# Two attention layers on one core: the readers of a projection's PSUM bank in another order, and one round of an input tile moved ahead

## Chip, cores and metric

One NeuronCore of a Trainium2 chip runs the whole program. The metric is device time in microseconds (us), from the launch to the end of one execution. TensorE is called PE here, VectorE DVE, ScalarE ACT, GpSimd POOL and SyncE SP, as in the profile.

## What is computed

Two attention layers over 2048 tokens, width 576, 32 heads of 18, whose outputs stand side by side. Layer A has one key head and one value head for all 32 query heads and attends to all tokens. Layer B is cut into four segments of 512 tokens. It attends causally inside a segment and adds what a linear memory of the earlier segments gives. A learned gate for each head mixes the two.

```python
def _A_ref(x, wq, wk, wv, wo):
    scores = einsum("bhqd,bkd->bhqk", q, k) * Dh ** -0.5
    o = einsum("bhqk,bkd->bhqd", softmax(scores), v)
    return o.reshape(B, S, H * Dh) @ wo

def _B_ref(x, wq, wk, wv, wo, beta):
    phi = lambda t: where(t > 0, t + 1.0, exp(t))
    g = sigmoid(beta)
    for s in range(4):                                   # segments
        a_dot = softmax(qs @ ks.T * scale + mask) @ vs   # causal
        a_mem = (phi(qs) @ M) / (phi(qs) @ z + 1e-6)
        o = g * a_mem + (1.0 - g) * a_dot
        M = M + phi(ks).T @ vs
        z = z + phi(ks).sum(over tokens)
    return o @ wo
```

## The kernel before

The program has two parts. The first, up to about 281 us, makes the projections: for A four chunks of 512 tokens (c), for B four segments (s). The second is the attention with the output projections. It walks through blocks of heads of A and B, and ACT makes the exponentials there.

**Tiles and rings.** A projection's output (heads times 18 rows, 512 tokens) is cut into five tiles t of up to 126 rows. PE makes a tile in one PSUM bank `pj` out of a ring of four, with 14 matmuls, since every operand is split in two fp32r parts (`wh`, `wl` and `xh`, `xl`) (proj, L252 to L259). Other PSUM names: `nd` (two banks, first half of the values), `tr` (one bank, transposes), `mm` (one bank, small sums).

**The readers of a bank.** In B's key tiles (L444 to L472) a bank has five readers, and the framework lets only one engine at a time read it. Before, they come in this order: DVE's maximum `kmB` (L454), ACT's copy `qp` (L124 in split2), DVE's subtraction that makes the second part of `qp` (L125), ACT's ramp, a Relu of the negated tile (L403 in phi), and, after ACT's exponential of it (L404), DVE's sum that makes the features `kf` or `qf` (L406). PE then transposes the features (`natural`, L422, tile `tr`) and DVE copies them out (L423).

**Weights that are still being loaded.** Segment 0 does something more in its key tiles: the last five parts (10 to 14) of B's weights, those of the query projection, are split there. In tile t, ACT rounds part 10 + t out of its buffer `wr` (L249 in split_wpart), POOL subtracts (L250), and POOL then issues the load of the next part (L240 in load_wpart):

```python
if s == 0:
    split_wpart(10 + t)
    if t < 4:
        load_wpart(11 + t)
```

All five steps are held in program order on their engines (`pin`, which is tc.keep_in_program_order). So the load of part 11 + t stands on POOL's queue behind POOL's subtraction of part 10 + t, and that stands behind ACT's rounding of part 10 + t.

**The gate.** Behind the fifth part POOL issues seven small loads of the gate's argument `gt` (L479). ACT takes its exponential (L550), and DVE finishes it (L551 to L553).

**What sets the order.** In the first part, what is not pinned is put in order by the framework's scheduler when the program is built. Each engine then runs its fixed list from the front and waits at the first instruction whose inputs are not there. The attention part has an order written out by hand.

**The next segment's x.** `next_x` and `load_xk` (L199 to L219) load and round the next segment's input: in segment 0 on DVE (`behind=True`: cast, then subtraction), in segments 1 and 2 on ACT and POOL (`aside=True`). Three buffers `xr` hold the raw input.

Of the kernel before, what the change touches and what calls it, by code (L numbers as in the profile page):

```python
# [14 lines left out]
ALU = mybir.AluOpType  # L15
AX = mybir.AxisListType
# [61 lines left out]
def attention_pair_kernel(ctx, tc, a_xT, a_w, a_wo, b_xT, b_w, b_wo, b_beta, ident_d, hmask_d, bmask_d, cmask_d, sel_d, zmask_d, selx_d, sely_d, out):  # L78
    nc = tc.nc
# [37 lines left out]
    fm = cp.tile([128, 5], F32, name="fm")  # L117
    nc.gpsimd.memset(fm, 0.0)

    def split2(pool, src, R, hold=lambda ins: ins):  # L120

        n = src.shape[-1]
        qp = pool.tile([128, 2, C], F32R, name="qp", bufs=3)
        hold(nc.scalar.copy(qp[:R, 0, :n], src))  # L124
        hold(nc.vector.tensor_tensor(qp[:R, 1, :n], src, qp[:R, 0, :n].bitcast(F32), op=ALU.subtract))  # L125
        return qp

    def store_parts(qp, r0, R, dst, h0, nh):
        nc.sync.dma_start(dst[h0 : h0 + nh].rearrange("h d j t -> (h d) j t"), qp[r0 : r0 + R].bitcast(F32))
# [30 lines left out]
    with ExitStack() as ph:  # L160
# [109 lines left out]
        for c in range(NCH):  # L270
            ready = {}
            if c == 0:

                for k in range(5):
                    load_part(raw[0][:, k, :CA], a_w, 0, CA, k, nc.sync)
                    load_part(xraw(0, k), a_xT, 0, C, k, nc.sync if k else nc.scalar)
                for k in range(5):
                    load_part(xraw(1, k), a_xT, C, C, k, nc.sync)
                nc.sync.dma_start(ident, ident_d)
                xh, xl, fillx = next_x(a_xT, 0)  # L280
                nx = next_x(a_xT, 1)
                for t in TILES:
                    ready[t] = ps.tile([128, C], F32, name="mm", bufs=1) if t == 3 else ps.tile([128, C], F32, name="pj", bufs=4)
                for k in range(5):
                    fillx(k)
                    split_w(wAh, wAl, raw[0][:, k, :CA], 0, CA, k, nc.vector)
                    parts_ = [(wAh, xh), (wAh, xl), (wAl, xh)] if k < 4 else [(wAh, xh), (wAl, xh)]
                    for i, (w, x) in enumerate(parts_):
                        for t in TILES:
                            M = 114 if t == 4 else 126  # L290
                            nc.tensor.matmul(  # L291
                                ready[t][:M],
                                w[:, k, 126 * t : 126 * t + M],
                                x[:, k],
                                start=k == 0 and i == 0,
                                stop=k == 4 and i == 1,
                            )
                for k in range(5):
                    nx[2](k)
            else:  # L300
                xh, xl = nx[:2]
                nx = next_x(a_xT, c + 1) if c < NCH - 1 else next_x(b_xT, 0)
                if c == 2:
                    wBl, wBh = (pw.tile([128, 5, WB], F32R, name=n) for n in ("wBl", "wBh"))
            for t in TILES:
                M = 114 if t == 4 else 126
                if c == 0:
                    pj = ready[t]
                else:

                    nm, bufs = ("nd", 2) if c == 1 and t == 4 else ("pj", 4)
                    pj = ps.tile([128, C], F32, name=nm, bufs=bufs)
                    proj(pj[:M], wAh, wAl, xh, xl, 126 * t, M)
                R = RT[t]
                if t == 4:
                    nc.vector.tensor_reduce(km[:M, c : c + 1], pj[:M], axis=AX.X, op=ALU.max, apply_absolute_value=True)
                    vT = p1.tile([128, C], F32, name="vT", bufs=2)
                    nc.scalar.copy(vT[96:114], pj[96:114])
                if t == 0:

                    pv = ps.tile([128, 4, 128], F32, name="tr", bufs=1)
                    for i in range(4):
                        nc.tensor.transpose(pv[:, i, 0:DH], vT[96:114, 128 * i : 128 * i + 128], ident[96:114, 96:114])
                    nc.vector.tensor_copy(VAv[:, 4 * c : 4 * c + 4, 1:VW], pv[:, :, 0:DH])
                nc.scalar.activation(AQ[:R, t, c * C : c * C + C], pj[:R], AF.Abs)
                R2 = 90 if t == 4 else 126
                if (c, t) == (NCH - 1, 3):
                    lastq = pj
                else:
                    qp = split2(pt, pj[:R2], R2)  # L330
                    store_parts(qp, 0, R, qA[c], H0[t], HT[t])
                if c == 0:
                    load_part(xraw(2, t), a_xT, 2 * C, C, t, nc.sync)
                if c:
                    nx[2](t)

                i = 5 * (c - 2) + TILES.index(t)
                if i >= 0:
                    split_wpart(i)
                    if i + 4 < 10 or i == 8:  # L340
                        load_wpart(i + 4 if i < 8 else 10)
                if t == 4:
                    nc.sync.dma_start(kA[:, :, c * C : c * C + C], qp[72:90].bitcast(F32))
            if c == 0:
                for i in range(4):
                    load_wpart(i)
                pin(nc.gpsimd.dma_start(hmask[:126], hmask_d))
                pin(nc.gpsimd.dma_start(bmask[:126], bmask_d))
                pin(nc.gpsimd.dma_start(sel[:114], sel_d))
                pin(nc.gpsimd.dma_start(zmask[:126], zmask_d))  # L350
                pin(nc.gpsimd.dma_start(selx[:126], selx_d))
                pin(nc.gpsimd.dma_start(sely, sely_d))
                pin(nc.gpsimd.dma_start(ones_d.rearrange("j (a b) -> (j a) b", b=128), onest))
# [43 lines left out]
        nc.gpsimd.memset(mz, 0.0)  # L397
        zc = p2.tile([128, 5], F32, name="zc")

        def phi(src, R, nm, bufs, hold=lambda ins: ins):  # L400

            e = p2.tile([128, C], F32, name="ph_e", bufs=2)
            hold(nc.scalar.activation(e[:R], src, AF.Relu, scale=-1.0))  # L403
            hold(nc.scalar.activation(e[:R], e[:R], AF.Exp, scale=-1.0))  # L404
            f = p2.tile([128, C], F32, name=nm, bufs=bufs)
            hold(nc.vector.scalar_tensor_tensor(f[:R], src, 0.0, e[:R], op0=ALU.max, op1=ALU.add))  # L406
            return f

        for s in range(NSEG):
# [34 lines left out]
            for t in range(5):  # L444
                if s == t == 0:
                    pj = ahead
                else:
                    pj = ps.tile([128, C], F32, name="pj", bufs=4)
                    proj(pj[:126], wBh, wBl, xh, xl, 630 + 126 * t if t < 4 else 504, 126)
                if t and not last:  # L450
                    natural(f, pkN[:, t - 1, :, 0:126], 0, 126)

                hold = (lambda ins: ins) if last else pin
                hold(nc.vector.tensor_reduce(kmB[:126, t : t + 1], pj[:126], axis=AX.X, op=ALU.max, apply_absolute_value=True))  # L454
                qp = split2(pt, pj[:126], 126, hold)
                if t < 4:
                    store_parts(qp, 0, 126, kB[s], 7 * t, 7)
                    hold(nc.vector.tensor_scalar(kbB[:126, t], zmask[:126, t], kmB[:126, t : t + 1], None, op0=ALU.mult))
                else:
                    store_parts(qp, 0, 72, qB[s], 28, 4)  # L460
                    store_parts(qp, 72, 54, kB[s], 28, 3)
                    magnitude(4, pj)
                if not last or t == 4:
                    f = phi(pj[:126], 126, "kf" if t < 4 else "qf", 2 if t < 4 else 5, hold)
                    if t == 4:
                        fs[4] = f
                if s and not last:
                    nx[2](t, aside=True)
                if s == 0:
# [3 lines that stand above are left out]
# [59 lines left out]
            if not last:  # L532
                for i in range(4):
                    values(i, 1)

            for t in range(4):
                pj = ps.tile([128, C], F32, name="pj", bufs=4)
                proj(pj[:126], wBh, wBl, xh, xl, 126 * t, 126)
                magnitude(t, pj)
                qp = split2(pt, pj[:126], 126)  # L540
                store_parts(qp, 0, 126, qB[s], 7 * t, 7)
                if s == 0:
                    nx[2](t, behind=True)
                    if t == 3:
                        nx[2](4, behind=True)
                if s:
                    fs[t] = phi(pj[:126], 126, "qf", 5)
                    from_memory(t)
                if (s, t) == (1, 1):
                    nc.scalar.activation(gt, gt, AF.Exp, scale=-1.0)  # L550
# [970 lines left out]
```

## Time and profile before

| what | value |
|---|---|
| device time, median of 3 runs | 1398.94 us (1397.28 to 1399.08) |
| device time of the profiled execution | 1397.32 us |
| its span, first to last instruction | 1395.4 us |
| PE busy in the span | 1382.5 us (99%) |
| ACT busy in the span | 1204.4 us (86%) |
| DVE busy in the span | 1033.2 us (74%) |
| POOL busy in the span | 261.1 us (19%) |
| granted PE clock | 0.999 |

About 1.9 us of the time lies outside the span. Matmuls are pipelined and overlap in the rows, so a busy PE means only that the next matmul had begun before the one ahead had drained. The step from one start to the next is what a matmul costs. A bracket at the end of a timeline row tells how long the engine sat idle before the instruction and who released it. An x14 at the end of a row means so many instructions in one row.

### The profile page before, as it was taken

To read this page: it belongs to the slowest core of one execution; us is meant where nothing else is said; L and a number is where in the kernel's file an instruction comes from. 1 tells how busy PE (TensorE), PEld (TensorE's weight loads), DVE (VectorE), ACT (ScalarE), POOL (GpSimd) and SP (SyncE) were. 2 spreads that over 40 slices of the span, in tenths; PEclk is the share of its full clock that TensorE was granted. 3 is DMA by queue.
4 is the path that set the end of the run, shared out by engine and by line. 5 is a ranking of instruction groups with operands and counts; after the bars stand their busy time and mean duration, and the time that the engine had idled before them with its cause. 6 is when DMAs were issued, how large, how long until landed. Compare 5 with 4: busy or idle time off the path is not lost.

```text
span 1395.4 us, 41198 instructions
## 1 busy us (share of the span) xinstructions
PE 1382.5 (99%) x17455; PEld 835.6 (60%) x17455; DVE 1033.2 (74%) x1512; ACT 1204.4 (86%) x1494; POOL 261.1 (19%) x382
## 2 busy tenths in 40 slices
PE   9999999999999999999999999999999999999998
PEld 6787887755554555555555555555555555555558
DVE  6655454477787788787888877876879778887884
ACT  4543553499999999999999999999999999999992
POOL 2443221003312211412110122113010220001002
PEclk9999999999999999999999999999999999999999
DMA  9766656576465445332312452232103321120013
GB/s 288 259 216 196 191 178 206 175 210 189 146 182 172 139 149 158 101 113 78 112 59 71 141 160 56 91 115 83 52 34 94 111 76 39 32 73 21 18 63 133
DMA packets 89022, 173.67 MB, mean 124 GB/s; under 512 B 12308, under 2 KB 20621, under 8 KB 88402
## 3 DMA queue, kind: packets, MB, share of 16 engines
q1 hardware_dynamic: 81902, 159.22, 36.6%
q0 software_dynamic: 2176, 6.51, 1.6%
q10 hardware_dynamic: 4752, 5.23, 1.1%
q8 instruction: 139, 2.28, 0.7%
q14 instruction: 53, 0.43, 0.1%
HBM read 99.65 MB, written 70.67 MB: 122 GB/s over the span
## 4 chain that ended last, share of the span: by engine, by line
PE 88%; DVE 5%; ACT 4%; issue 2%; DMA 1%; SPq 0%; POOL 0%; DVEq 0%; ACTq 0%
PE O L938 32%; PE E L890 20%; PE F L741 11%; PE pj L259 11%; ACT P L908 4%; PE E L898 3%; PE nd L496 2%; PE pj L496 2%; DVE W L905 2%; PE E L1222 2%; PE pj L291 1%; PE F L797 1%; PE tr L422 0%; DVE sm L690 0%; DMA stB<-qB 0%
## 5 line engine op out<-in xcount | busy, mean ns | idle before, releaser
L908 ACT ACTIVATE P<-E 128x1024 f32<-128x1024 f32 (+1 forms) x800 | 788.1, 1076 | 1.6 <-PE E L890 1.3
L905 DVE COPY W<-E 128x1024 f32<-128x1024 f32 (+2 forms) x416 | 453.2, 1089 | 143.1 <-PE E L890 84.2
L938 PE MATMUL O<-P,VA 128*32 128x256 f32 x7504 | 507.1, 379 | 0.0
L908 ACT ACTIVATE P<-W 128x1024 f32<-128x1024 f32 (+1 forms) x330 | 369.9, 1121 | 6.3 <-DVE W L905 5.6
L938 PEld LDWEIGHTS O<-P,VA 128*32 128x32 f32 x7504 | 259.0, 110 | 137.7 <-issue 4.3
L890 PE MATMUL E<-xl,kstA 56*128 56x512 f32 x1920 | 317.2, 430 | 2.1 <-ACT P L908 1.9
L890 PEld LDWEIGHTS E<-xl,kstA 56*128 56x128 f32 x1920 | 155.0, 184 | 159.1 <-issue 94.8
L913 POOL TENSOR_SCALAR_AFFINE_SELECT P<-P 128x256 f32<-128x256 f32 (+1 forms) x192 | 95.0, 495 | 412.5 <-ACT P L908 403.3
L725 POOL TENSOR_TENSOR xh<-xh,rb 126x512 f32<-126x512 f32 (+1 forms) x55 | 72.9, 1350 | 425.9 <-DVE PD L871 185.1
L741 PE MATMUL F<-woB,xh 126*32 126x192 f32 (+1 forms) x1920 | 126.6, 338 | 0.0
L938 PE MATMUL O<-PD,VA 128*32 128x256 f32 x688 | 88.9, 379 | 0.0
L741 PEld LDWEIGHTS F<-woB,xh 126*32 126x32 f32 (+1 forms) x1920 | 38.6, 108 | 74.9 <-issue 69.9
L938 PE MATMUL O<-P,vseg 128*32 128x256 f32 (+2 forms) x1536 | 81.4, 344 | 0.1
L947 DVE COPY oe<-O 128x512 f32<-128x512 f32 x64 | 44.3, 692 | 42.3 <-PE O L938 40.4
L259 PE MATMUL pj<-xh,wBl 128*126 128x512 f32 x180 | 71.9, 400 | 0.4 <-issue 0.4
L864 DVE TENSOR_SCALAR PD<-E 128x512 uint32<-128x512 f32 x86 | 59.2, 688 | 17.6 <-PE E L890 15.8
L259 PE MATMUL pj<-xh,wBh 128*126 128x512 f32 x180 | 71.6, 398 | 0.5 <-DVE xh L219 0.5
L124 ACT CAST qp<-pj 126x512 fp32r<-126x512 f32 (+1 forms) x54 | 31.1, 585 | 46.9 <-DVE kmB L454 41.8
L741 PE MATMUL F<-woA,xh 126*32 126x192 f32 (+1 forms) x960 | 63.9, 338 | 0.0
L938 PEld LDWEIGHTS O<-P,vseg 128*32 128x32 f32 x1536 | 48.8, 109 | 24.4 <-issue 1.9
L898 PE MATMUL E<-stB 56*128 56x256 f32 (+3 forms) x512 | 61.5, 348 | 2.0 <-ACT P L908 1.5
L871 DVE SCALAR_TENSOR_TENSOR PD<-PD,q 128x512 f32<-128x512 f32 x86 | 59.5, 692 | 3.0
(228 smaller groups left out, 1544.0 us busy)
## 6 DMA issues: line engine op xcount, KB each, us to landing
stB<-kB SPq DMA_DIRECT2D x96, 144.0 KB
stB<-qB SPq DMA_DIRECT2D x32, 288.0 KB
xl<-qA SPq DMA_DIRECT2D x30, 288.0 KB
oA<-oe SPq DMA_DIRECT2D x32, 256.0 KB
oB<-oe SPq DMA_DIRECT2D x32, 256.0 KB
qA<-qp SPq DMA_DIRECT2D x16, 504.0 KB
kB<-qp SPq DMA_DIRECT2D x16, 504.0 KB
qB<-qp SPq DMA_DIRECT2D x16, 504.0 KB
```

What stands on the lines that cost most here:

```text
L259: nc.tensor.matmul(dst, w[:, c0 : c0 + M], x, start=i == 0, stop=i == len(ops) - 1)
L496: nc.tensor.matmul(pj[:, :n], x, w, start=m == 0, stop=m == len(ops) - 1)
L725: ins = tc.keep_in_program_order(nc.gpsimd.tensor_tensor(dst, a, b, op=op))
L741: nc.tensor.matmul(dst[32 * j : 32 * j + 32], parts[ab, c][: RT[t], t, r0 : r0 + 32], wo[ab][: RT[t], t, c0 : c0 + n], start=start, stop=stop,
L864: v.tensor_scalar(y, e, EXP_A, EXP_B, op0=ALU.mult, op1=ALU.add)
L871: lambda: stt(p, p, POLY[3], w, op0=ALU.add, op1=ALU.mult),
L890: nc.tensor.matmul(e[:, j], kstA[rows, 128 * kt : 128 * kt + 128], st[rows, h, :], start=True, stop=True)
L898: nc.tensor.matmul(e[:, j, c0 : c0 + 512 - 128 * k], st[rows, 4 + h, ks], st[rows, h, 128 * k :], start=True, stop=True)
L905: gate.append(nc.vector.tensor_copy(src[:, hs, :n], e[:, hs, :n]))
L908: nc.scalar.activation(p[:, hs, :n], src[:, hs, :n], AF.Exp, scale=SCALE)
L913: nc.gpsimd.affine_select(diag, diag, pattern=[[0, 2], [0, m], [1, 128]], base=0, channel_multiplier=-1, compare_op=ALU.is_ge, fill=0.0)
L938: nc.tensor.matmul(o[32 * j : 32 * j + 32, q0 : q0 + n], v, p[:, j % 2, p0 : p0 + n], start=m == hf == 0, stop=last and hf == 1,)
```

## The change

Three things are moved, and no instruction is added or taken away.

1. The readers of a bank in B's key tiles come in the order copy, ramp, subtraction, features, maximum. The ramp (now in a function `negative`) is issued between copy and subtraction through a hook in split2. Tile 4 and the query tiles of segments 1 to 3 get the same order of copy, ramp, subtraction, features; ACT's absolute value (`magnitude`) stays ahead of the copy in the query tiles and behind the subtraction in tile 4. The last segment's key tiles 0 to 3 have no features; there only the maximum moves behind the split.
2. In A's tile 4 the maximum `km` comes after copy and subtraction.
3. In segment 0 the next segment's x is rounded one tile sooner: tile 0 ahead of the loop over query tiles, tile t + 1 in turn t.

```diff
+    def split2(pool, src, R, hold=lambda ins: ins, between=lambda: None):
...
         hold(nc.scalar.copy(qp[:R, 0, :n], src))
+        between()
         hold(nc.vector.tensor_tensor(qp[:R, 1, :n], src, qp[:R, 0, :n].bitcast(F32), op=ALU.subtract))
...
                 if t == 4:
-                    nc.vector.tensor_reduce(km[:M, c : c + 1], pj[:M], axis=AX.X, op=ALU.max, apply_absolute_value=True)
                     vT = p1.tile([128, C], F32, name="vT", bufs=2)
...
+                if t == 4:
+                    nc.vector.tensor_reduce(km[:M, c : c + 1], pj[:M], axis=AX.X, op=ALU.max, apply_absolute_value=True)
...
-        def phi(src, R, nm, bufs, hold=lambda ins: ins):
+        def negative(src, R, hold=lambda ins: ins):
 
             e = p2.tile([128, C], F32, name="ph_e", bufs=2)
             hold(nc.scalar.activation(e[:R], src, AF.Relu, scale=-1.0))
+            return e
+
+        def phi(src, R, nm, bufs, hold=lambda ins: ins, e=None):
+
+            e = e or negative(src, R, hold)
             hold(nc.scalar.activation(e[:R], e[:R], AF.Exp, scale=-1.0))
...
                 hold = (lambda ins: ins) if last else pin
-                hold(nc.vector.tensor_reduce(kmB[:126, t : t + 1], pj[:126], axis=AX.X, op=ALU.max, apply_absolute_value=True))
-                qp = split2(pt, pj[:126], 126, hold)
+                e = []
+                between = (lambda: None) if last and t < 4 else lambda: e.append(negative(pj[:126], 126, hold))
+                qp = split2(pt, pj[:126], 126, hold, between)
                 if t < 4:
                     store_parts(qp, 0, 126, kB[s], 7 * t, 7)
-                    hold(nc.vector.tensor_scalar(kbB[:126, t], zmask[:126, t], kmB[:126, t : t + 1], None, op0=ALU.mult))
...
-                    f = phi(pj[:126], 126, "kf" if t < 4 else "qf", 2 if t < 4 else 5, hold)
+                    f = phi(pj[:126], 126, "kf" if t < 4 else "qf", 2 if t < 4 else 5, hold, e[0])
...
+                hold(nc.vector.tensor_reduce(kmB[:126, t : t + 1], pj[:126], axis=AX.X, op=ALU.max, apply_absolute_value=True))
+                if t < 4:
+                    hold(nc.vector.tensor_scalar(kbB[:126, t], zmask[:126, t], kmB[:126, t : t + 1], None, op0=ALU.mult))
...
+            if s == 0:
+                nx[2](0, behind=True)
             for t in range(4):
...
-                qp = split2(pt, pj[:126], 126)
+                e = []
+                qp = split2(pt, pj[:126], 126, between=lambda: e.append(negative(pj[:126], 126)) if s else None)
...
-                    nx[2](t, behind=True)
-                    if t == 3:
-                        nx[2](4, behind=True)
+                    nx[2](t + 1, behind=True)
...
-                    fs[t] = phi(pj[:126], 126, "qf", 5)
+                    fs[t] = phi(pj[:126], 126, "qf", 5, e=e[0])
```

The scheduler answers the new program order with new lists for the engines. Three places of them follow. The changed file has other line numbers: L250 is there the rounding that was L249, L405 and L411 are ramp and exponential (L403 and L404), L429 the transposes (L422), L260 the projection's matmul (L259), L561 the gate's exponential (L550), L512 to L515 the values (L502 to L505). Numbers behind a name tell buffers apart: `pj_888`, `pj_924` and `pj_960` are segment 0's key tiles 1, 2 and 3, `wr_886` and `wr_922` hold weight parts 11 and 12.

ACT in segment 0, from key tile 1 on, before:

```order
L124 CAST qp_910<-pj_888 126x512
L403 ACTIVATE ph_e_915<-pj_888 126x512
L404 ACTIVATE ph_e_915<-ph_e_915 126x512
L249 CAST wBh_483<-wr_886 128x504
L124 CAST qp_946<-pj_924 126x512
L502 COPY vch_1041<-nd_1044 128x16x18
L504 COPY kn_1043<-nd_1044 128x18
L505 DMA vB0_73<-vch_1041 128x304
L403 ACTIVATE ph_e_951<-pj_924 126x512
L404 ACTIVATE ph_e_951<-ph_e_951 126x512
L249 CAST wBh_483<-wr_922 128x504
```

The same place after the change:

```order
L124 CAST qp_909<-pj_888 126x512
L405 ACTIVATE ph_e_911<-pj_888 126x512
L411 ACTIVATE ph_e_911<-ph_e_911 126x512
L250 CAST wBh_483<-wr_886 128x504
L124 CAST qp_945<-pj_924 126x512
L405 ACTIVATE ph_e_947<-pj_924 126x512
L411 ACTIVATE ph_e_947<-ph_e_947 126x512
L250 CAST wBh_483<-wr_922 128x504
L124 CAST qp_981<-pj_960 126x512
```

The values' copies (L502 to L505) have left this stretch. The rounding of each weight part stands, as before, between one key tile's exponential and the next tile's copy.

PE around the transposes of key tile 2's features (`kf_954` before), before; `nd_1086` is the third block of the values' first half:

```order
L496 MATMUL nd_1086<-wBh_483,xh_636 128x306
L496 MATMUL nd_1086<-wBh_483,xl_637 128x306
L422 MATMUL tr_975<-ident_118,kf_954 128x126 x4
L496 MATMUL nd_1086<-wBl_482,xh_636 128x306
L496 MATMUL nd_1086<-wBh_483,xh_636 128x306
```

The same transposes after (`kf_952`); `pj_997` is key tile 4:

```order
L260 MATMUL pj_960<-xh_636,wBh_483 126x512
L260 MATMUL pj_960<-xh_636,wBl_482 126x512
L429 MATMUL tr_975<-ident_118,kf_952 128x126 x4
L260 MATMUL pj_997<-xh_636,wBh_483 126x512
L260 MATMUL pj_997<-xl_637,wBh_483 126x512
```

They moved from 50 matmuls behind key tile 3 to right behind it. In the same way tile 0's transposes now stand in the middle of tile 2, tile 1's behind the fourth matmul of tile 3, tile 3's behind tile 4, and tile 4's behind the 25th matmul of the values. Those of segment 0's tile 4 and of `kn` left the query projection for the values.

ACT around the gate's exponential, before; `pj_1192` is the last block of the values' second half, `pj_1209` and `pj_1234` are query tiles 0 and 1:

```order
L502 COPY vch_1041<-pj_1192 128x16x18
L505 DMA vB0_73<-vch_1041 128x304
L124 CAST qp_1129<-tr_1122 18x512
L428 ACTIVATE aq_1224<-pj_1209 126x512
L124 CAST qp_1226<-pj_1209 126x512
L550 ACTIVATE gt_121<-gt_121 128x7
L428 ACTIVATE aq_1249<-pj_1234 126x512
```

After; `pj_1141` and `pj_1158` are the first two blocks of the values' second half:

```order
L535 ACTIVATE ph31_1133<-ph31_1133 128x72
L561 ACTIVATE gt_121<-gt_121 128x7
L124 CAST qp_1129<-tr_1122 18x512
L512 COPY vch_1041<-pj_1141 128x16x18
L515 DMA vB0_73<-vch_1041 128x304
L512 COPY vch_1041<-pj_1158 128x16x18
```

The gate's exponential moved from behind query tile 0 to ahead of all four copies of the values' second half.

## Rows read from the trace of the kernel before

**Rows 1.** Stretches: us, busy of PE, PEld, DVE, ACT, POOL; clock, DMA share, GB/s

```profile
0.00:281.00 281.00, 278.02 (x1846) 224.38 (x1846) 151.28 (x272) 125.20 (x253) 73.74 (x114) 1.00 0.67 214
...
840.00:1120.00 280.00, 279.65 (x4074) 152.51 (x4078) 222.89 (x311) 278.65 (x319) 51.97 (x71) 1.00 0.26 79
```

**Rows 2.** PE's waits, 0 to 281 us: us in total, times, longest

```profile
PE tr L422 <- DVE kf L406: 0.7, 1, 0.7
PE pj L259 <- DVE xh L219: 0.5, 1, 0.5
PE pj L259 <- issue: 0.4, 1, 0.4
```

**Rows 3.** POOL's timeline, segment 0: start, duration, instruction, idle before

```profile
83.24 0.35 POOL L485 MEMSET vch<- 128x128 f32 x1
85.81 1.27 POOL L250 TENSOR_TENSOR wBl<-wr,wBh 128x504 fp32r<-128x504 f32 x1 [2.22 <-ACT wBh L249]
87.02 0.57 POOL L240 DMA_DIRECT2D wr<-b_w  x1
...
110.01 1.26 POOL L250 TENSOR_TENSOR wBl<-wr,wBh 128x504 fp32r<-128x504 f32 x1 [4.46 <-ACT wBh L249]
111.22 4.40 POOL L479 DMA_DIRECT2D gt<-b_beta  x7
```

**Rows 4.** Weight loads, parts 11, 12, 13, 14: KB, us from issue to landing

```profile
wr<-b_w POOLq DMA_DIRECT2D x1, 252.0 KB, 4.7
...
wr<-b_w POOLq DMA_DIRECT2D x1, 252.0 KB, 2.9
...
wr<-b_w POOLq DMA_DIRECT2D x1, 252.0 KB, 3.3
...
wr<-b_w POOLq DMA_DIRECT2D x2, 126.0 KB, 2.6
```

**Rows 5.** ACT's timeline, key tiles 0 to 2 of segment 0

```profile
82.54 0.59 ACT L124 CAST qp<-pj 126x512 fp32r<-126x512 f32 x1 [6.78 <-DVE kmB L454]
83.96 0.60 ACT L403 ACTIVATE ph_e<-pj 126x512 f32<-126x512 f32 x1 [0.84 <-DVE qp L125]
84.60 0.63 ACT L404 ACTIVATE ph_e<-ph_e 126x512 f32<-126x512 f32 x1
85.14 0.60 ACT L249 CAST wBh<-wr 128x504 fp32r<-128x504 f32 x1
...
91.77 0.61 ACT L249 CAST wBh<-wr 128x504 fp32r<-128x504 f32 x1 [0.90 <-DMA wr<-b_w]
93.79 0.59 ACT L124 CAST qp<-pj 126x512 fp32r<-126x512 f32 x1 [1.40 <-DVE kmB L454]
```

**Rows 6.** DVE's timeline: features of key tile 0

```profile
85.26 0.69 DVE L406 SCALAR_TENSOR_TENSOR kf<-pj,ph_e 126x512 f32<-126x512 f32 x1 [1.26 <-ACT ph_e L404]
```

**Rows 7.** PE's timeline, segment 0 (single matmuls at marked places)

```profile
81.91 0.39 PE L259 MATMUL pj<-xh,wBh 128*126 128x512 f32 x1
...
85.17 0.39 PE L259 MATMUL pj<-xh,wBh 128*126 128x512 f32 x1
...
86.32 0.59 PE L422 MATMUL tr<-ident,kf 126*128 126x126 f32 x4
...
86.99 0.39 PE L259 MATMUL pj<-xh,wBh 128*126 128x512 f32 x1
...
109.03 0.39 PE L259 MATMUL pj<-xh,wBh 128*126 128x512 f32 x1
...
123.42 0.40 PE L568 MATMUL nd<-aq,kbB 126*32 126x512 bf16 x3
```

**Rows 8.** PE's timeline, first and 36th matmul of the values

```profile
92.51 0.30 PE L496 MATMUL nd<-wBh,xh 128*128 128x306 f32 x1
...
97.45 0.30 PE L496 MATMUL nd<-wBh,xl 128*128 128x306 f32 x1
```

**Rows 9.** ACT's timeline: the gate's exponential and the next instruction

```profile
120.92 0.21 ACT L550 ACTIVATE gt<-gt 128x7 f32<-128x7 f32 x1 [6.25 <-DMA gt<-b_beta]
```

More of the change, by code (lines that the diff above doesn't have):

```diff
@@ L118, in attention_pair_kernel @@
     nc.gpsimd.memset(fm, 0.0)
-    def split2(pool, src, R, hold=lambda ins: ins):
+    def split2(pool, src, R, hold=lambda ins: ins, between=lambda: None):
         n = src.shape[-1]
```

## The prediction

> **What bounds the kernel now.** I read the busy times by stage first. In the projections (0 to 281 us) PE is busy 278.0 of 281 us and no other engine is near that; in the attention, as from 840 to 1120 us, ACT is busy 278.65 of 280 us [rows 1]. So the projections end when PE has worked off its list, and the attention after them runs at ACT's pace and has nothing to catch up with: what the projections gain or lose arrives at the end one to one. Next come PE's waits in the projections. Beside the start there are three: 0.7 us for key features `kf`, 0.5 us for the last tile of the second x, 0.4 us without a cause the profile shows [rows 2]. That is all that moving readers can win. The question is therefore what the new order makes PE wait for.
>
> The answer lies in segment 0, in a loop that runs through three engines. ACT rounds a weight part, POOL subtracts it, POOL issues the load of the next part, and ACT's next rounding needs that load. From subtraction to issue 1.21 us pass (85.81 to 87.02) [rows 3]; landing takes 4.7, 2.9 and 3.3 us for parts 11 to 13 and 2.6 us for the halves of part 14 [rows 4]; from rounding to subtraction 0.67 us (85.14 to 85.81). One round is thus 4.8 to 6.6 us. Before, this loop is nearly hidden: ACT idled once for it, 0.90 us ahead of 91.77 [rows 5], because PE's list let 50 matmuls pass before it needed key tile 2's features.
>
> **The change part by part.**
>
> *Reader order in the key tiles.* From a tile's copy to its transposes the chain is now copy to ramp 0.54 us (the step from 84.60 to 85.14 between two independent ACT instructions), ramp to exponential 0.64, exponential to features 0.66 (84.60 to 85.26), the features' 0.69 [rows 5, 6], and about 0.1 to PE: 2.6 us. The maximum's 0.7 us ahead of the copy and the wait between subtraction and ramp are gone. In itself that is a gain. But the scheduler has moved the transposes up to match it, and ACT's rounding of the weight part still stands between one tile's exponential and the next tile's copy. PE now meets the loop.
>
> I follow segment 0. POOL's set-up ends at 83.59 as before (83.24 and 0.35), so the subtraction of part 10 starts there instead of at 85.81 and load 11 is issued at 84.8 [rows 3]. This load went out into busy queues before and took 4.7 us; it goes out at nearly the same moment now, so I take 4.7: it lands at 89.5. ACT has finished tile 1's exponential near 84 and stands before that rounding until 89.5. Tile 2's copy, queued behind it, starts at 90.0, and its features reach PE at 92.6. PE starts tile 2 at 81.91 and one tile takes 3.26 us (to 85.17); a group of transposes costs 0.44 (0.67 from 86.32 to 86.99, less one matmul's 0.23) [rows 7]. With two groups ahead, PE is through tile 3 at 85.17 + 0.88 + 3.26 = 89.3. **It waits 3.3 us.**
>
> Part 12: 89.5 + 0.67 + 1.21 + 2.9 = 94.3; tile 3's copy at 94.8, features at 97.4. PE is there at 92.6 + 0.44 + 3.26 = 96.3: **1.1 us.** Part 13: 94.3 + 0.67 + 1.21 + 3.3 = 99.5; tile 4's copy at 100.0 and, with its absolute value in between, features at 103.1. PE has then done one group of transposes and 25 value matmuls at 0.14 us (35 steps from 92.51 to 97.45) [rows 8]: 97.4 + 0.44 + 3.5 = 101.3, **1.8 us.** Part 14, in two halves 0.57 us apart: 99.5 + 0.67 + 1.21 + 0.57 + 2.6 = 104.6, subtraction at 105.2.
>
> The landings bound this from both sides: 2.6 us for all, the shortest, and 4.7 us for all, the longest. I keep the measured one for each part, since the queues at 84.8 are those of 87.0, and the later parts go out, as before, after the x loads are through.
>
> The Trainium skill speaks against the 4.7: its page "DMA: Bandwidth & Descriptors", section "Anatomy of one DMA — SWDGE (gpsimd) path", gives about 2.0 us plus the bytes over 436 GB/s, an estimate of 2.6 us for 252 KB. The four rows are at or above that, by up to 2.1 us, so it works here as a floor.
>
> *The gate.* Its loads stand on POOL behind part 14's subtraction. From that subtraction to the end of ACT's wait 10.9 us pass (110.01 to 120.92) [rows 3, 9]. Before, ACT waited 6.25 us there behind query tile 0, and the ring of four banks covered it. Now ACT stands there ahead of the four copies that free the banks of the values' second half, and query tile 0 needs the first of them. The gate is there at 105.2 + 10.9 = 116.1; then follow the gate's exponential, one rounding and the copy, about 1.1 us: query tile 0 can start at 117.2. PE's own list brings it there at 109.03 + 3.3 + 1.1 + 1.8 + 0.9 (two groups of transposes that came later before) = 116.1 [rows 7]. So the gate adds 1.1 us, and **the query projection starts at 117.2 instead of 109.03, 8.2 us late.**
>
> *What comes back.* From there to the sum over `aq` it took 14.4 us (109.03 to 123.42); without transposes in it 56 matmuls take 13.0 [rows 7]: 1.4 us less. DVE, no longer pushed back by the gate's 6.25 us in the middle of the query tiles, is not late at the turn to segment 1, so the waits of 0.7 and 0.5 us go [rows 2]: 1.2 us less.
>
> *Second x sooner, and A's maximum.* One cast and one subtraction move out of the end of the query tiles into a stretch where DVE has nothing queued; the saving is within the 1.2 us. Their loads are SP's and change places with stores there only by one tile. A's maximum goes behind a copy that waited for it; PE waited for neither in A [rows 2], so nothing; if that cover were gone it would be one maximum, 0.7 us, per chunk. In segments 1 and 2 the place of the weight part is taken by a rounding of x whose load lies three buffers ahead; a tile's 3.26 us cover the 2.6 us chain, so I count nothing. Without that cover each of eight tiles could cost some tenths; that is in the upper end.
>
> **Sum:** 8.2 - 1.4 - 1.2 = 5.6 us more. On the profiled execution's 1397.32 us that is 1402.9; on the median of the runs, 1.6 us above it, 1404.5. I forecast the middle, 1403.7 us.
>
> **The rivals.**
>
> *The loads land fast.* With 2.9 us for each of parts 11 to 13 the three waits are 1.5, 1.1 and 1.3 us, the gate comes at 113.8, and the same sum gives 3.4 us: 1400.7 to 1402.3. For it: two of three landings are near that. Against: load 11's was 4.7. By the skill's 2.6 us for every load (same page) the sum is 2.5 us, 1399.8 us on the profiled execution.
>
> *The loads land slowly.* The loop now runs against other stores and x loads. With 4.7 us for every load the waits are 3.3, 2.9 and 3.1 us, part 14 comes 5 us later and the gate with it: 10.9 us more, 1408.2 to 1409.8; 4.0 us for each gives 8.1.
>
> *It ends no slower: the loop stays hidden and only the gain is left.* The waits of 0.7 and 0.5 us go, perhaps the 0.4 too: 1.2 to 1.6 us less, 1395.7 to 1396.1 on the profiled execution. This decides at one point: PE wants tile 2's features at 89.3, hence the copy at 86.7, hence load 11 landed 1.4 us after its issue at 84.8. No load of a part came under 2.6 us [rows 4]. It would also hold if ACT got to tile 2's copy ahead of that rounding; the order on the engine says otherwise.
>
> **How the numbers follow.** Forecast, 4 to 7 us more: 0.52. Fast loads: 0.22. Slow loads: 0.18. Hidden loop: 0.08. A difference under 0.2% (2.8 us) is about what a measurement of this kernel cannot tell from none. Forecast and slow loads lie above that, and half of the fast ones: 0.81 slower. The other half and most of the hidden loop, whose gain is under 0.2%: 0.16 the same. The rest, 0.03, faster. The range goes from the shortest landings, 1399.8, to slow loads at about 4.0 to 4.4 us for each, 1408.5.
>
> **What would show it.** In the profile after: PE waiting in segment 0 for `kf` two to three times, over 1 us each; ACT idle some 5 us before the second weight rounding, released by the load of `wr`; ACT's wait for the gate ending near 116 us with PE waiting for a copy of the values behind it; query tile 0 near 117 us; no wait of PE for `xh` at the turn to segment 1. I am wrong if PE has no wait for `kf` there, or if segments 1 and 2 show waits too.

## The result, and the profile after

The changed kernel takes 1404.83 us (median of 6 runs, 1403.45 to 1408.52), the kernel before 1399.01 us beside it: a ratio of 1.0046, 95% interval 1.0032 to 1.0060, 5.8 us slower. The forecast was 1403.7. The profiled execution took 1404.13 us, its span is 1402.2 against 1395.4: 6.8 us more.

First the stretches, with the columns of [rows 1]:

```profile
0.00:281.00 281.00, 274.24 (x1809) 222.24 (x1810) 146.99 (x265) 123.95 (x251) 73.41 (x114) 0.99 0.65 207
840.00:1120.00 280.00, 279.63 (x4086) 152.38 (x4075) 223.51 (x312) 278.61 (x319) 48.85 (x68) 1.00 0.27 81
```

The attention is as before. In the projections PE is busy 274.24 us of the same 281, where it was 278.02 [rows 1]. PE's waits up to 290 us (total, times, longest; the 1.1 us for `gt` is at the very start and was there before) tell where it idled:

```profile
PE tr L429 <- DVE kf L413: 3.0, 2, 2.8
PE tr L429 <- DVE qf L413: 1.2, 1, 1.2
PE nd L175 <- DVE gt L486: 1.1, 1, 1.1
PE pj L260 <- ACT vch L512: 0.8, 1, 0.8
PE nd L506 <- ACT kn L514: 0.4, 1, 0.4
```

The waits of [rows 2] are gone, and new ones stand in segment 0: 2.8 us for key features, 1.2 us for query features, 0.4 and 0.8 us for copies of the values. The chain of waits from 80 to 125 us, in order of time (start, us, what), shows what they hang on:

```profile
83.58 1.21 POOL wBl L251
84.79 4.59 DMA wr<-b_w
...
89.40 0.62 ACT wBh L250
...
90.10 1.19 POOL wBl L251
91.29 3.44 DMA wr<-b_w
...
94.76 0.62 ACT wBh L250
...
96.67 3.35 DMA wr<-b_w
...
102.48 4.28 DMA wr<-b_w
...
106.79 0.62 ACT wBh L250
...
108.75 3.58 POOL gt L489 x6
112.33 5.98 DMA gt<-b_beta
...
119.43 5.60 PE pj L260 x23
```

This is a ring through three engines: POOL subtracts a weight part (L251) and issues the next load, the load lands, ACT rounds it (L250), POOL subtracts again. It turns four times, then the seven loads of `gt` follow, and query tile 0 starts at 119.43 instead of 109.03 [rows 7]. Before, ACT idled 0.90 us for one such load [rows 5]. Its timeline now has 5.62 us ahead of the rounding of part 11, and query tile 0's bank comes free by the copy behind the exponential of `gt`:

```profile
89.40 0.61 ACT L250 CAST wBh<-wr 128x504 fp32r<-128x504 f32 x1 [5.62 <-DMA wr<-b_w]
...
118.42 0.21 ACT L561 ACTIVATE gt<-gt 128x7 f32<-128x7 f32 x1 [6.92 <-DMA gt<-b_beta]
...
118.99 0.38 ACT L512 COPY vch<-pj 128x288 f32<-128x288 f32 x1
```

The ring itself hasn't become slower. Part 11 was rounded at 91.77 before [rows 5] and is rounded at 89.40 now. Part 14 is rounded at 106.79 now, and before it came at 109.32 (ACT's timeline of the kernel before):

```profile
109.32 0.60 ACT L249 CAST wBh<-wr 128x504 fp32r<-128x504 f32 x1
```

What changed is PE's list: it wants each tile's features right behind the next tile, and the value matmuls that filled this time before now come later.

What comes back is read from single rows of PE's timeline: the sum over `aq` in segments 0, 1 and 2, and the first matmul of the attention:

```profile
132.62 0.40 PE L579 MATMUL nd<-aq,kbB 126*32 126x512 bf16 x3
...
183.50 0.40 PE L579 MATMUL nd<-aq,kbB 126*32 126x512 bf16 x3
...
234.39 0.40 PE L579 MATMUL nd<-aq,kbB 126*32 126x512 bf16 x3
...
287.43 0.74 PE L901 MATMUL E<-st,kstA 56*128 56x512 f32 x4
```

The same rows of the kernel before, from segment 1 on:

```profile
175.80 0.40 PE L568 MATMUL nd<-aq,kbB 126*32 126x512 bf16 x3
...
226.66 0.40 PE L568 MATMUL nd<-aq,kbB 126*32 126x512 bf16 x3
...
280.37 1.06 PE L890 MATMUL E<-st,kstA 56*128 56x512 f32 x4
```

Query tile 0 is 10.4 us late, the sum of segment 0 9.2 (123.42 before [rows 7]), those of segments 1 and 2 7.7 each, the attention 7.1, the end 6.8.

### The profile page after: what moved, and what is told of

Read it like the earlier page. It is cut to its first block, busy times and chain, and to the rows that moved or that the text cites. A ratio compares the mean times of both kernels' runs of the same rounds, so it can differ in the third digit from the quotient of the medians.

```text
span 1402.2 us, 41204 instructions
## 1 busy us (share of the span) xinstructions
PE 1385.4 (99%) x17455; PEld 838.0 (60%) x17455; DVE 1033.4 (74%) x1512; ACT 1203.4 (86%) x1494; POOL 259.9 (19%) x382
## 4 chain that ended last, share of the span: by engine, by line
PE 87%; ACT 4%; DVE 4%; DMA 2%; issue 2%; POOL 1%; SPq 0%; DVEq 0%; ACTq 0%; POOLq 0%
PE O L949 32%; PE E L901 20%; PE F L752 11%; PE pj L260 11%; ACT P L919 4%; PE E L909 3%; DVE W L916 2%; PE nd L506 2%; PE E L1233 2%; PE pj L506 1%; DMA wr<-b_w 1%; PE pj L292 1%; PE F L808 1%; DMA stB<-qB 0%; POOL wBl L251 0%
## 5 line engine op out<-in xcount | busy, mean ns | idle before, releaser
L126 DVE TENSOR_TENSOR qp<-pj,qp 126x512 fp32r<-126x512 f32 (+1 forms) x54 | 36.9, 686 | 55.7 <-ACT ph_e L405 40.0
L260 PE MATMUL pj<-xh,wBh 128*126 128x512 f32 x180 | 74.0, 411 | 0.8 <-ACT vch L512 0.8
L260 PE MATMUL pj<-xh,wBl 128*126 128x512 f32 x180 | 72.0, 400 | 0.0
```

Source lines behind the costliest of these rows:

```text
L260: nc.tensor.matmul(dst, w[:, c0 : c0 + M], x, start=i == 0, stop=i == len(ops) - 1)
```

## The experiments

The theory: the ring of part loads, hidden before, delays PE, because ACT's rounding stands between key tiles whose features PE's new list wants at once, and `gt` behind its end adds a little. Rivals: the second x; the readers' order itself, with features that come late; the wait for `gt`; PE's clock. Each kernel was timed beside its own runs of the kernel before (medians 1398.0 to 1398.5 us), so ratios, or distances to these medians, are the fairer measure between kernels timed at different times.

### Which part of the change: the readers alone, the second x alone

Readers alone (the changed kernel with the second x as before):

```diff
-            if s == 0:
-                nx[2](0, behind=True)
             for t in range(4):
...
                 if s == 0:
-                    nx[2](t + 1, behind=True)
+                    nx[2](t, behind=True)
+                    if t == 3:
+                        nx[2](4, behind=True)
```

> The changed kernel with one part of the change undone: the second x of B is rounded after each of B's query tiles again, as before; the readers keep their new order. Theory (the loop of part loads, stretched by the readers' order, then the gate's exponential, makes the loss): PE, ScalarE and GpSimd keep the changed kernel's lists, so the profile again shows the wait of about 2.8 us for kf in segment 0 and query tile 0 at about 119.4; time 1404 to 1405 us, 5 to 7 us above before. Rival (the earlier rounding of the second x holds up VectorE and the tiles behind it): back to within 1 us of before, about 1399 us.

The second x alone is the reverse of these lines in the kernel before.

> The kernel before with the other part alone: the second x of B is rounded a tile sooner, the readers stay in the old order. Theory: nothing is lost, and the wait of 0.5 us for xh at the turn to segment 1 is gone: 1398.0 to 1399.0 us, 0 to 0.5 us below before. Rival (this part carries the loss): 1404 to 1405 us, 5 us or more above before.

Measured: the readers alone 1404.80 us, 1.0042 (1.0026 to 1.0059); the second x alone 1398.22 us, 0.9996 (0.9986 to 1.0007). The loss is all the readers'. The second x did not take away the wait for `xh` as I had expected: 0.3 us of 0.5 stayed, and the wait for `kf` beside it grew from 0.7 to 1.1. With the readers alone the wait for `xh` is gone.

The readers-alone profile settles something else by the way. PE's waits up to 290 us:

```profile
PE tr L429 <- DVE kf L413: 4.1, 3, 2.4
PE tr L429 <- DVE qf L413: 2.4, 1, 2.4
```

And PE in two stretches of the same kernel (length, PE busy, granted clock, DMA share, GB/s):

```profile
92.00:96.00 4.00, 3.86 (x18) 1.00 0.64 196
...
104.00:108.00 4.00, 4.00 (x19) 0.59 0.48 150
```

Here key tile 4 ran at full clock, and the second wait for `kf` (1.46 us) that I had forecast is there. In the changed kernel's own profile it is not: the granted clock fell behind the 2.8 us wait, as the same view shows:

```profile
92.00:96.00 4.00, 3.47 (x11) 0.50 0.63 194
96.00:100.00 4.00, 4.00 (x17) 0.68 0.44 120
```

0.50 is the lower of the two levels, 1.2 GHz. Between the transposes at 92.53 and 99.03 PE was busy with key tile 4 where it would else have waited for the ring. Behind it PE still waited 1.2 us for `qf`, so the ring set its pace again. Query tile 0 came at 119.43 there and at 118.85 here.

### Opening the ring

Each load of parts 11 to 14 is issued one split sooner, from the same two buffers:

```diff
                         load_wpart(i + 4 if i < 8 else 10)
+                    if i == 9:
+                        load_wpart(11)
...
                     split_wpart(10 + t)
-                    if t < 4:
-                        load_wpart(11 + t)
+                    if t < 3:
+                        load_wpart(12 + t)
```

> The changed kernel with the loads of weight parts 11 to 14 each issued one split sooner (part 11 behind the split of part 9, part 12+t behind that of 10+t), from the same two buffers. The loads then run ahead of the key tiles and the ring of rounding, subtraction, load and next rounding is open; the order of the readers is untouched. Theory (the ring makes the loss): no wait of 2.8 us for kf in segment 0, part 12 rounded near 89.4, gate near 107 and query tile 0 near 110 where the changed kernel has 118.4 and 119.4; what is left of the change is its small gains, so about 1397.3 us, 7.5 us below the changed kernel and 1.7 below before, with 1395.5 to 1399.5 allowed. Rival (the readers' order itself costs the time, by features that come late): the wait for kf stays and the time stays at 1403 to 1405 us.

The same edit in the kernel before:

> The kernel before with the loads of weight parts 11 to 14 each issued one split sooner, the same edit as for the changed kernel. Theory: in the kernel before the loads already land ahead of the roundings that read them, so the earlier issue finds nothing to shorten: 1398 to 1399 us, within 0.5 us of before. Rival (earlier loads are a gain in any order of the readers, and did not undo the change but covered it): 1390 to 1393 us, 5 to 8 us below before.

Measured: the changed kernel with earlier loads 1397.44 us, 0.9990 (0.9980 to 1.0001), 7.4 us below the readers alone on the same chip; measured again, 1396.79 us, 0.9986 (0.9977 to 0.9994). The kernel before with earlier loads 1397.48 us, 0.9997 (0.9987 to 1.0006): nothing. So the loads aren't a gain of their own clear of noise; they undo what the readers' order did, and with it gone the order is at most a small gain (the interval of the first measurement holds 1, that of the second doesn't). The rows that follow are from the second measurement. The first one's profiled execution (1400.11 us, the slowest of its twelve) shows a wait of 2.2 us for `xl` in layer A, ahead of the ring, that has no part in this account. PE's waits for features in segment 0:

```profile
PE tr L431 <- DVE qf L415: 0.3, 1, 0.3
PE tr L431 <- DVE kf L415: 0.2, 1, 0.2
```

ACT's timeline, the rounding of part 12 and the exponential of `gt`:

```profile
90.14 0.61 ACT L250 CAST wBh<-wr 128x504 fp32r<-128x504 f32 x1 [2.71 <-DMA wr<-b_w]
...
109.42 0.21 ACT L563 ACTIVATE gt<-gt 128x7 f32<-128x7 f32 x1 [5.52 <-DMA gt<-b_beta]
```

PE's timeline, the first matmul of query tile 0 and the sum over `aq` in segment 1:

```profile
111.13 0.39 PE L260 MATMUL pj<-xh,wBh 128*126 128x512 f32 x1
...
175.09 0.40 PE L581 MATMUL nd<-aq,kbB 126*32 126x512 bf16 x3
```

The wait of 2.8 us is gone. The roundings came later than I expected (90.1 for 89.4, `gt` at 109.4 for 107): two loads under way at once took 5.0 and 6.1 us each (issued at 85.12 and 87.28, rounded at 90.14 and 93.40). PE had work enough to cover that. Query tile 0 is still 2.1 us later than before (109.03), in part because more transposes stand ahead of it, but the sum of segment 1 is 0.7 us sooner (175.80 before). No run left the ring closed and put PE's transposes back behind the values, so that cure is untried.

### The wait for `gt`

```diff
-                    nc.scalar.activation(gt, gt, AF.Exp, scale=-1.0)
+                    pin(nc.scalar.activation(gt, gt, AF.Exp, scale=-1.0))
```

holds the exponential at its place in the program, behind query tile 1 of segment 1.

> The changed kernel with the gate's exponential held at its place in the program, in segment 1 behind query tile 1, so that no copy of ScalarE in segment 0 stands behind the seven gate loads. Theory (the ring has already put PE's own list at about 118.6 when the gate lets the copies go at 118.4): query tile 0 moves by 0.8 us only, the time is 0.5 to 1.2 us below the changed kernel, about 1403.8 us. Rival (the wait for the gate's loads is the main loss, and without it the PE would catch up what the ring took): 1399 to 1400 us, 4 to 6 us below the changed kernel.

Measured: 1403.73 us (1402.31 to 1404.40), 1.0034 (1.0023 to 1.0045), 1.1 us below the readers alone on the same chip, with intervals that overlap. The rival falls: `gt` is not the main loss. In its profiled execution query tile 0 starts at 119.45, no sooner than in the changed kernel, since the ring ran later there: part 14 was rounded at 107.86 instead of 106.79. From that rounding to query tile 0 it is 11.6 us instead of 12.6, so by these two executions the gate's place cost about 1 us. PE's waits, and ACT's rounding of part 14:

```profile
PE tr L429 <- DVE kf L413: 3.4, 2, 3.2
PE tr L429 <- DVE qf L413: 2.4, 1, 2.4
...
PE nd L506 <- ACT kn L514: 0.9, 1, 0.9
...
107.86 0.61 ACT L250 CAST wBh<-wr 128x504 fp32r<-128x504 f32 x1 [3.38 <-DMA wr<-b_w]
```

Both edits together in the changed kernel, and both in the kernel before:

> The changed kernel with the earlier part loads and with the gate's exponential held in segment 1 as well. Theory: with the ring open the gate (at about 107) opens before PE's list reaches the tiles behind it, so nothing is added: within 0.7 us of the changed kernel with earlier loads alone, about 1397.4 us. Rival (the gate still holds up copies of the last tiles): 1 to 2 us less, 1395.5 to 1396.5 us.

> The kernel before with the earlier part loads and with the gate's exponential held in segment 1, the same two edits that made the changed kernel about 2 us faster than before. Theory (what is left of the change, once its ring is open, is a gain of 1 to 2 us by the readers' order, and the two edits by themselves do nothing): within 0.7 us of before, 1397.3 to 1398.7 us, 1.5 to 2 us above the changed kernel with both. Rival (the two edits are the gain, in any order of the readers): 1395.5 to 1396.5 us, as the changed kernel with both.

Measured: 1395.87 us, 0.9985 (0.9976 to 0.9994), in the changed kernel; 1397.32 us, 0.9997 (0.9985 to 1.0008), in the kernel before. The first lay in the rival's range against the 1397.44 measured before on another chip, so the two changed kernels were run side by side:

> The changed kernel with the earlier part loads alone, measured again beside the one with the gate held as well. Theory (the gate behind seven landings holds up copies of ScalarE, but no matmul waits for them): within 0.7 us of the kernel with both, 1395.5 to 1396.8 us. Rival (the gate costs by itself): 1 to 2 us above it, about 1397.4 us.

> The changed kernel with the earlier part loads and the gate held in segment 1, measured again. Theory and rival both: about 1396 us, 1.5 to 2.5 us below before; what tells them apart is the distance to the kernel with the loads alone, under 0.7 us for the theory and 1 to 2 us for the rival.

Measured: 1396.79 and 1396.17 us, 0.9986 and 0.9984. The distance of 0.6 us is inside the theory's bound and inside the intervals, so with the ring open no cost of `gt` is clear of noise. Side by side both beat the kernel before, by 1.7 and 2.3 us. The two edits without the readers' order lie 1.2 us below it by medians, but their interval holds 1 (one of their runs took 1405.13 us). So what the readers' order adds to the same two edits is 1.2 us by medians, where 1.5 to 2 were expected, and that isn't clear of noise.

### A longer ring

```diff
                     split_wpart(10 + t)
+                    pin(nc.gpsimd.tensor_tensor(wBl[:, t, 0:504], wrs[10 + t], wBh[:, t, 0:504].bitcast(F32), op=ALU.subtract))
```

> The changed kernel with each of GpSimd's subtractions of weight parts 10 to 14 done twice (the same values are written again), in front of the next part's load: about 1.2 us more in each of four to five rounds of the ring. Theory: the ring sets when query tile 0 starts, so four rounds add 4 x 1.2 = 4.8 us to the wait of TensorE, of which the later stages give a part back: 3 to 5.5 us above the changed kernel, 1407.5 to 1410 us. Rival (GpSimd is idle there and the ring has slack): within 0.5 us of the changed kernel.

Measured: 1408.99 us (1408.72 to 1409.63), 1.0079 (1.0065 to 1.0092), 4.2 us above the changed kernel, or 5.2 when each is taken beside its own runs of the kernel before. ACT's roundings in its timeline, and the gate's exponential:

```profile
91.47 0.61 ACT L250 CAST wBh<-wr 128x504 fp32r<-128x504 f32 x1 [7.89 <-DMA wr<-b_w]
...
98.23 0.61 ACT L250 CAST wBh<-wr 128x504 fp32r<-128x504 f32 x1 [4.50 <-DMA wr<-b_w]
...
105.05 0.61 ACT L250 CAST wBh<-wr 128x504 fp32r<-128x504 f32 x1 [4.56 <-DMA wr<-b_w]
...
126.94 0.21 ACT L562 ACTIVATE gt<-gt 128x7 f32<-128x7 f32 x1 [7.51 <-DMA gt<-b_beta]
```

A round takes 6.8 us instead of 5.3 (94.76 to 100.04), and query tile 0 starts at 124.45, 5.0 us later. These 5.0 us are not the added work alone. The scheduler made other lists here: the gate's exponential stands behind the first copy of the values' second half and no longer holds up query tile 0, while part 14 is rounded 7.4 us later (114.21). The direction and the rough size speak for the ring: POOL is busy for 73 of the 281 us of this stage in the changed kernel, yet of 5.0 us of work put into the ring (four rounds of 1.25 us) 4 to 5 us arrive at the end.

### Is the half clock a cost of its own?

Twelve unread matmuls on PE, first ahead of the transposes of key tile 3 (`t == 4`), then a tile sooner (`t == 3`):

```diff
+                if s == 0 and t == 4:
+                    pz = ps.tile([128, C], F32, name="mm", bufs=1)
+                    for _ in range(12):
+                        pin(nc.tensor.matmul(pz[:126], wBh[:, 0, 630:756], xh[:, 0], start=True, stop=True))
                 if t and not last:
                     natural(f, pkN[:, t - 1, :, 0:126], 0, 126)
```

> The changed kernel with twelve matmuls whose result nobody reads put on TensorE ahead of the transposes of kf of segment 0 that it waits for, so that it works through part of the wait of 2.8 us and its granted clock may stay at full speed behind it. Theory (the ring sets the start of query tile 0, and the half speed of key tile 4, 5.8 us in place of 3.3, only takes the place of the next wait): key tile 4 takes about 3.3 us, a wait of about 1 to 2 us for kf of tile 3 comes back, and the time is within 0.7 us of the changed kernel. Rival (the half clock is a cost of its own): 2 to 3 us below the changed kernel, about 1402 us.

> The changed kernel with twelve matmuls whose result nobody reads (12 x 0.23 us) put on TensorE directly behind key tile 3, so that it works through its long wait for kf of segment 0; in the kernel with the filler a tile later they stood behind the half-clock stretch. Theory (the ring of part loads sets the start of query tile 0, and the half clock only fills time that TensorE would wait): key tile 4 runs at full granted clock in about 3.3 us, waits of 1 to 1.5 us for kf of tile 3 and about 2.4 us for qf come back, query tile 0 at 118.5 to 119.5, the time within 0.7 us of the changed kernel, 1403.8 to 1405.2 us. Rival (the half clock is a cost of its own, 14 matmuls x 0.2 us): 2 to 3 us below the changed kernel, 1401.5 to 1402.5 us.

Measured: 1407.15 us, 1.0069 (1.0055 to 1.0082), and 1409.77 us, 1.0078 (1.0066 to 1.0090). Both theory and rival missed, twice. The first filler stood in the wrong place, behind key tile 4: PE went through them from 98.31 to 101.06, query tile 0 came at 120.40, 1.0 us late, and 1.9 us more were lost ahead of a `pj` matmul of the last segment, for which the profile names no cause. The second did what it was meant to. PE in three stretches:

```profile
92.00:96.00 4.00, 4.00 (x20) 1.00 0.65 194
...
104.00:108.00 4.00, 1.79 (x10) 0.67 0.36 125
108.00:112.00 4.00, 4.00 (x17) 0.50 0.32 83
```

PE's waits in the same kernel:

```profile
PE tr L429 <- DVE qf L413: 2.3, 1, 2.3
PE nd L510 <- ACT kn L518: 2.1, 1, 2.1
PE tr L429 <- DVE kf L413: 1.7, 2, 1.5
```

Key tile 4 ran at full clock and waits of 1.5 and 2.3 us came back, as expected. But then PE waited 2.1 us more, for a copy that stands on ACT behind the rounding of part 14. That wait is not the fillers' doing alone. In both kernels with fillers the scheduler put the first copy of the values behind this rounding; in the changed kernel it stands ahead of it, and PE waited 0.4 us at this place. ACT's timeline in the changed kernel, then in the second one with fillers:

```profile
103.41 0.38 ACT L512 COPY vch<-nd 128x288 f32<-128x288 f32 x1
...
106.73 0.39 ACT L516 COPY vch<-nd 128x288 f32<-128x288 f32 x1
```

The clock fell at that wait: 18 matmuls of the values ran at 0.255 us instead of 0.14, 2.1 us that no later wait of PE took up. Query tile 0 started at 122.02, 2.6 us later than in the changed kernel. So half clock ahead of a further wait for the ring cost nothing in these executions, and half clock behind the last such wait did. What the fillers would have done with the copies in their old place isn't shown, so whether half clock is a cost of its own stays open. The Trainium skill ("TensorE: Matmul & The Clock Gate", section "Why this matters for your kernels") advises against idle gaps between bursts of matmuls; the fall behind 2.8 us of idle agrees. Here the kernel with unread matmuls in the gap, and with the copies moved, was about 5 us slower than the changed kernel, and taking the cause of the gap away gained 7.

## Why the prediction was right, step by step

| step | forecast | measured |
|---|---|---|
| load 11 issued, part 11 rounded | 84.8, 89.5 | 84.79, 89.40 |
| PE's first wait for `kf`, transposes at | 3.3, 92.6 | 2.78, 92.53 |
| part 12 rounded (landing) | 94.3 (2.9) | 94.76 (3.44) |
| PE's second wait for `kf` | 1.1 | none; key tile 4 at half clock |
| part 13 rounded | 99.5 | 100.04 |
| PE's wait for `qf` | 1.8 | 1.23 |
| part 14 rounded (landing of its second half) | 104.6 (2.6) | 106.79 (4.28) |
| `gt` after part 14's subtraction | 10.9 | 10.9 |
| query tile 0 | 117.2 (+8.2) | 119.43 (+10.4) |
| won back to the end | 2.6 | 3.6 |
| profiled execution | +5.6 | +6.8 |

The mechanism was right: the ring that PE's new list meets, the place of the first wait, `gt` adding about 1 us at its end (0.84), and the two waits of [rows 2] gone. The earlier loads, the longer ring and the late `gt` each tested one of these, the earlier loads most cleanly.

Three terms were mis-sized. The largest is part 14's landing. I took the 2.6 us of [rows 4], but its second half took 4.28 us by the chain; together with part 12's 3.44 for 2.9 this accounts for 2.2 of the 2.3 us by which `gt` and query tile 0 were late. Its first half took 2.7 us, about what the halves took before; why the second took longer no run shows. A landing read in the kernel before need not hold for the moment to which the load is moved. (The Trainium skill's estimate of 2.6 us for 252 KB, from "DMA: Bandwidth & Descriptors", section "Anatomy of one DMA — SWDGE (gpsimd) path", again works as a floor: 4.59, 3.44 and 3.35 us here.) Second, the half clock of key tile 4 was in no step; it took the place of the wait of 1.1 us and part of the 1.8. Third, more came back than forecast: 1.2 us up to the sum of segment 0 (forecast 1.4), 1.5 at the turn to segment 1 (1.2), and 0.7 between the sum of segment 2 and the attention, plus 0.3 behind that, which I had not counted. The first error and the third partly cancelled; on medians, 5.8 us, the sum of 5.6 looks better than its terms.

For the second x the size was right, within the 1.2 us, but not the mechanism: the wait for `xh` goes with the readers' order, with or without it. The prediction's reason for that, a VectorE held back by the gate, is borne out in part: the kernel before with both edits has no wait for `xh` either, while its wait for `kf` grew to 1.0 us; with the earlier loads alone both waits stayed (0.4 and 0.7 us).

Of the rivals, the hidden loop fell where the prediction put its turning point: load 11 would have had to land 1.4 us after its issue and took 4.59. The landings of parts 11 to 13 lay between the fast and the slow case.

What stays open: the idle of 0.4 to 1.9 us ahead of a `pj` matmul late in the projections, which some kernels show and for which the profile names nothing; and where the spread of the changed kernel's runs (1403.45 to 1408.52) comes from, since only one execution has a trace. The slowest run has the lowest granted clock, 0.995, and the fastest the highest, 0.999, which speaks for the place where the clock falls; but the landing of load 11, too, differs from kernel to kernel, 4.2 to 5.1 us from the same place.

## What to carry to other kernels

When readers are moved so that one engine's list becomes tighter, look for a ring of a few buffers that runs through the same engines (round, subtract, load, round) and was hidden by the old slack; add up one turn and compare it with the work between two needs. Here the cure was to issue each load one step sooner from the same buffers, which turned 5.8 us of loss into a gain of about 1 to 2 us over the kernel before. Don't fill a wait to hold up the clock before asking whether the wait itself can go, and whether the clock would only fall somewhere dearer.

## What the hardware showed unexpectedly

PE's granted clock fell to 0.50 behind a wait of 2.8 us in the changed kernel, for about 6 us; behind 3.2 us in the kernel with the late `gt` it fell too and was back after about 3 us. Behind 2.4 us it did not fall in the readers-alone kernel, but it did there behind the third wait (2.4, 1.5 and 2.4 us).

One and the same load, part 11 issued at 84.6 to 85.0, took 4.2 to 5.1 us in five kernels (the changed one, the readers alone, the late `gt` and the two with fillers). Two part loads under way at once took 5.0 and 6.1 us from issue to the rounding that waited for them. The first of these is within what a single load took, so only the second hints at a price of the company.
